# Forgetting attention and a tanh-shrink MLP on one core: half-feature order for unit 0, a subtraction on GpSimd, merged selectors, a q copy on VectorE and one step moved

## The chip, the cores and the metric

The kernel runs on one core of a Trainium2 chip. The metric is the device time of one execution in microseconds (us). Times inside an execution are counted from the start of the profiled span. Engines: PE is TensorE (PEld its weight loads), DVE is VectorE, ACT is ScalarE, POOL is GpSimd, SP is SyncE. A trailing q (SPq, POOLq) is the engine's sequencer, which issues DMAs.

## What is computed

Eight batches of eight heads, 576 positions, head size 64, in float32. The output of the attention becomes rows of 512 features for a two-layer MLP.

```python
scores = scale * q @ k.T                       # scale = 1/8
cum    = cumsum(log(clip(f, 1e-4, 1)))         # per head, over positions
scores = where(causal, -1e9, scores + cum[i] - cum[j])
attn   = softmax(scores)                       # rows divided by sum + 1e-9
x      = (attn @ v) as [4608, 512]             # batch and position, head and feature
h      = x @ w_in                              # 2048 features
out    = (h - tanh(h)) @ w_out                 # [4608, 512]
```

## The kernel before

**Order.** Each engine executes its instructions in the order in which the program writes them; the order is written by hand. The attention goes by pairs of heads of one batch (32 pairs, numbered 0 to 31; pairs 0 to 3 are batch 0, 4 to 7 batch 1), and the MLP by units of 512 rows (9 units, 0 to 8). The loop at the end of the kernel makes pass p: att_items(p) lists the attention's work for pair p, its seven score tiles t0 to t6 with what goes between them, and the loop puts TAKE[p] steps of the MLP between these items, as evenly as they go. Pass p also holds the values of pair p - 1, behind its tile t2.

**Scores and decay.** scores() makes one tile in a PSUM bank: a product over 67 rows, of which 64 are head features and three carry the decay, so that PE adds cum[i] - cum[j]. These three rows hold a high part (chi) and a low part (clo) of cum for the keys, a shifted cum (cq) for the queries, and constant rows of ones (ones16) and of a negative constant (minus16), against which chi and clo are multiplied. They reach the head layouts QT and KT by small DMAs: bulk() issues those of batch 0 on GpSimd (k_hi, q_hi and k_lo), load_aug() the others on SP. Pair 0 does not wait for them; it has its own layouts QS and KS, whose 88 rows include selector rows made from the columns of `per` (isb, isc, mul_*, add_*). Behind the product ScalarE takes the exponential of the tile (L367) into e; from batch 1 on GpSimd zeroes the part above the diagonal (L377, the mask). From batch 1 on the tiles use two PSUM banks in turn (ps_sc). Tile t3 takes the last keys of both heads, into el.

**Layouts of q and k.** trans() turns a pair's q or k on PE (L304) and copies the halves into QT and KT by VectorE and ScalarE (L317, L315). For pair 0 it is called with split=True, with four smaller copies (64x288); two are done at once and two returned as functions (q_rest, k_rest), which start() calls later. From batch 3 on, q and k are turned by DMA transposes on SP instead.

**Values.** values() multiplies the tiles with v (L395), VectorE divides (L404 to L406) into xn, and turn() brings xn into the MLP's layout XR: by PE in batch 0 (L423), by two DMA transposes on SP from batch 1 on (L429, L431). weights() prepares sums of quarters of w_out on VectorE (L284) in passes 8 to 10.

**MLP.** mlp1 makes 128 of the 2048 features for the 512 rows of a unit (L457, four products over 128 features of x, the last of which needs the last pair's xn), ScalarE takes the tanh (L462) and VectorE adds (L468) into gq. Unit 0's second product is mlp2_plain: sixteen steps s0 to s15, each eight products (L498) over one half of the features for 128 rows and half of the output. Four steps share one PSUM bank, which ScalarE copies (L503) and SP sends to memory. The later units use mlp2. Unit 1's first step needs xn of pairs 4 to 7.

**The start.** start() prepares pair 0. unread(n) makes n products of a constant tile that nobody reads. `late` holds the causal constants of batch 0, which PE adds to the scores (L361). The GpSimd queue also issues all loads of q, k, v, w_in (win) and w_out (wout), between its masks.

The step's order and the passes' shares before the change:

```python
e, mp, m, half = s // 8, s // 4 % 2, s // 2 % 2, s % 2
...
TAKE = (0, 0, 0, 0, 2, 7, 6, 6, 6, 8, 8, 7, 7)
```

Of the kernel before, what the change touches and what calls it, by code (L numbers as in the profile page):

```python
# [11 lines left out]
ALU = mybir.AluOpType  # L12
# [4 lines left out]
SHIFT = 5.0  # L17
# [4 lines left out]
def kernel(  # L22
# [10 lines left out]
    nc = tc.nc  # L33
# [3 lines left out]
    NH = B * H  # L37
# [7 lines left out]
    inv_qscale = float(D) ** 0.5  # L45
# [47 lines left out]
    qn, kn = ([t[0:S // NT6, :].rearrange("p (h n d) -> p h n d", h=H, n=NT6) for t in raw] for raw in (qraw, kraw))  # L93
# [42 lines left out]
    NX = NH + 3 * H  # L136
# [7 lines left out]
    id16 = cst.tile([P, P], FP16)  # L144
# [7 lines left out]
    ones16 = TK[0:NX, 0, :]  # L152
    nc.vector.memset(ones16, 1.0)
    minus16 = TK[0:2 * H, 1, :]
    nc.vector.memset(minus16, -1.0)
    late = cst.tile([P, P], FP16)
    nc.vector.memset(late, 0.0)
    nc.vector.memset(KT[0][:, :, S:PITCH], 0.0)
    chi = cst.tile([NX, S], FP16)
    clo = cst.tile([NH, S], FP16)  # L160
    cq = cst.tile([NH, S], FP16)
    KS = W1.rearrange("p k e -> p (k e)")[:, 0:2 * PITCH].rearrange("p (a n) -> p a n", a=2)
    QS = W2.rearrange("p k e -> p (k e)")[:, 0:2 * S].rearrange("p (a n) -> p a n", a=2)
    nc.vector.memset(KS[0:NX, :, S:PITCH], 0.0)
    per = cst.tile([NX, 9], FP32)
    nc.vector.memset(vn[0][D:P, NJ - 1, :, :], 0.0)
    isb, isc, mul_k, add_k, mul_l, mul_0, add_0, mul_1, add_1 = (per[:, i:i + 1] for i in range(9))
    EL = [cst.tile([P, 192], FP16, tag=f"el{i}", name=f"el{i}") for i in range(3)]
    load_v_rest(0)
    load_v_head(0, 0)  # L170
# [1 line left out]
    nc.gpsimd.affine_select(out=late, in_=late, compare_op=ALU.is_ge, fill=-60000.0,  # L172
                            base=0, pattern=[[1, P]], channel_multiplier=-1)

    def column(g, h):
        return id16[0:NX, NH + 3 * h + g:NH + 3 * h + g + 1]

    for to, g in ((isb, 1), (isc, 2)):
        nc.vector.tensor_reduce(out=to, in_=id16[0:NX, NH + g:NX:3], op=ALU.add, axis=mybir.AxisListType.X)
    nc.vector.tensor_scalar(out=mul_k, in0=isb, scalar1=-inv_qscale, scalar2=inv_qscale, op0=ALU.mult, op1=ALU.add)  # L180
    nc.vector.tensor_scalar_mul(out=add_k, in0=isb, scalar1=-1.0)
    nc.vector.tensor_scalar_mul(out=mul_l, in0=isc, scalar1=inv_qscale)
    for e in EL[0:2]:
        nc.vector.memset(e, 0.0)
    nc.vector.tensor_scalar(out=lf, in0=lf, scalar1=0.0001, scalar2=1.0,
                            op0=ALU.max, op1=ALU.min)
    nc.vector.memset(vn[0][:, :, :, D:VW], 1.0)
    for h, (mul, add) in enumerate(((mul_0, add_0), (mul_1, add_1))):
        nc.vector.tensor_scalar_mul(out=mul, in0=column(1, h), scalar1=inv_qscale)
        nc.vector.scalar_tensor_tensor(out=add, in0=mul, scalar=-SHIFT, in1=column(0, h), op0=ALU.mult, op1=ALU.add)  # L190
        nc.vector.tensor_tensor(out=add, in0=add, in1=column(2, h), op=ALU.subtract)
    nc.scalar.activation(out=lf, in_=lf, func=AF.Ln)
    nc.scalar.activation(out=expo, in_=lf[0:1, 0:1], func=AF.Exp)
    cum = TQ[0][0:NX, :, :].rearrange("p c s -> p (c s)").bitcast(FP32)[:, S:2 * S]
# [20 lines left out]
    def bulk():  # L215
        (k_hi, chi_0), (k_lo, clo_0), (q_hi, cq_0) = aug_rows(0)
        load_qk(qn, q, 0, 4, 6)
        load_qk(kn, k, 0, 4, 6)
        nc.gpsimd.dma_start(out=k_hi, in_=chi_0)
        nc.gpsimd.dma_start(out=q_hi, in_=cq_0)  # L220
        nc.gpsimd.dma_start(out=k_lo, in_=clo_0)
        load_qk(qn, q, 0, 6, H)
        load_qk(kn, k, 0, 6, H)
        for n in range(NJ - 1):
            load_v_block(0, n, 2, H)
# [264 lines left out]
        nc.vector.tensor_tensor(out=LHS[name](u, i)[:, ks], in0=LHS[x](u, i)[:, ks], in1=LHS[y](u, i)[:, ks], op=op)  # L490

    def mlp2_plain(u, s):
        e, mp, m, half = s // 8, s // 4 % 2, s // 2 % 2, s % 2
        if s % 4 == 0:
            M2[u] = bank("ops").rearrange("p (m e) -> p m e", m=2)
        ops, t0 = M2[u], (2 * mp + m) * P
        for ft in range(half * NK, half * NK + NK):
            nc.tensor.matmul(out=ops[:, m, :], lhsT=GQ[(u, ft % NK // 4)][:, half, ft % 4, t0:t0 + P],  # L498
                             rhs=wout[:, ft, e * HE:(e + 1) * HE], start=(m == 0 and ft == 0),
                             stop=(m == 1 and ft == NFT - 1), skip_group_check=True)  # L500
        if s % 4 == 3:
            ost = tmp.tile([P, DM], FP32, tag="ost", name="ost", bufs=3).rearrange("p (m e) -> p m e", m=2)
            nc.scalar.activation(out=ost, in_=ops, func=AF.Copy)  # L503
            r0 = u * UW + mp * 2 * P
            nc.sync.dma_start(out=out[r0:r0 + 2 * P, e * HE:(e + 1) * HE].rearrange("(m p) e -> p m e", p=P), in_=ost)
# [63 lines left out]
    def unread(n, lent=False):  # L569
        idle = m_bank("idle") if lent else ps_tr.tile([P, UW], FP32, tag="tr", name="idle")  # L570
        for i in range(n):
            nc.tensor.matmul(out=idle[:, i % 4 * P:i % 4 * P + P], lhsT=warm, rhs=warm, start=True, stop=True)
# [5 lines left out]
    def start():  # L578
        def row_q(h, mul, add):
            nc.scalar.activation(out=QS[NH:NX, h, :], in_=cum[NH:NX, :], func=AF.Identity, bias=add[NH:NX, :], scale=mul[NH:NX, :])  # L580

        unread(47)
        row_q(0, mul_0, add_0)
        q_rest = trans(*pairs[0], qn, (QS,), True, "AAAA", True)
        nc.scalar.activation(out=cq, in_=cum[0:NH, :], func=AF.Copy, bias=-SHIFT * inv_qscale, scale=inv_qscale)
        unread(6)
        k_rest = trans(*pairs[0], kn, (KS,), True, "VVVV", True)
        unread(38)
        q_rest[0]()
        scores(*pairs[0], 0)  # L590
        unread(4)
        nc.vector.scalar_tensor_tensor(out=clo, in0=cum[0:NH, :], scalar=inv_qscale, in1=chi[0:NH, :], op0=ALU.mult, op1=ALU.subtract)
        nc.vector.tensor_copy(out=KS[NH:NX, 1, 0:S], in_=KS[NH:NX, 0, 0:S])
        for fn in k_rest:
            fn()
        scores(*pairs[0], 1)
        row_q(1, mul_1, add_1)
        unread(4)
        q_rest[1]()
# [7 lines left out]
    def att_items(p):  # L607
        def put(fn, *args):
            items.append((lambda: fn(*args), True))

        items = []
        here = pairs[p] if p < len(pairs) else None
        before = pairs[p - 1] if 0 < p <= len(pairs) else None
        after = pairs[p + 1] if p + 1 < len(pairs) else None
        early = p < NPAIR
        for ti in range(len(TILES)):
            if here and (p > 0 or ti > 1):
                put(scores, *here, ti)
            if p == 1 and ti == 6:
                items.append((lambda: const_rows(1), False))  # L620
                items.append((lambda: load_aug(1), False))
            if p == 0 and ti in (0, 2, 5, 6):
                put(unread, {0: 2, 2: 14, 5: 4, 6: 6}[ti])
            if p == 1 and ti == 6:
                put(unread, 8, True)
            if p == 1 and ti == 3:
                put(last)
            for load in LOADS.get((p, ti), ()):
                items.append((load, False))
            at_q, at_k = (1, 3) if p == 0 else (0, 1) if early else (0, 2) if p == NPAIR else (0, 3)  # L630
            if p in (2 * NPAIR - 1, 2 * NPAIR, 2 * NPAIR + 1) and (ti % 2 or ti == 0):
                items.append((rest, False))
            if p in (2 * NPAIR - 1, 2 * NPAIR) and ti % 2 == 0:
                pair = pairs[2 * NPAIR + 2 * (p - 2 * NPAIR + 1) + ti // 4]
                put(trans, *pair, *((kn, KT) if ti % 4 else (qn, QT)), False, "VA")
            if ti == at_q and p < 2 * NPAIR - 1:
                put(trans, *after, qn, QT, early, "VV")
            if p == NPAIR:
                if ti in (4, 5):
                    put(mlp1, 0, ti - 4, 1)  # L640
            if ti == at_k and p < 2 * NPAIR - 1 and p != NPAIR:
                put(trans, *after, kn, KT, early, "AV" if early and p > 1 else "VV")
            if p == NPAIR:
                if ti == 1:
                    put(turn, *pairs[p - 2])
                    put(values, *before)
                    put(mlp1, 0, 0, 0)
                elif ti == 2:
                    put(mlp1, 0, 1, 0)
                    put(turn, *before)  # L650
                    put(trans, *after, kn, KT, early, "VV")
            elif early and ti in (2, 4) and before:
                put(values, *before, (ti // 2 - 1,))
            elif not early and ti == 2 and before:
                put(values, *before, (0, 1), p == NPAIR + 2)
            if p < NPAIR:
                if ti == 1 and p > 1:
                    put(turn, *pairs[p - 2], True)
            elif p > NPAIR and ti == 3:
                items.append((release, False))  # L660
                put(turn, *before)
        return items
# [1 line left out]
    mlp = [(mlp1, u, s) if s < NFT else (mlp2_plain if u < PLAIN else mlp2, u, s - NFT)  # L664
           for u in range(NU) for s in range(2 * NFT if u < PLAIN else NFT + 2 * len(STEPS))]
    mlp = mlp[2:]
    TAKE = (0, 0, 0, 0, 2, 7, 6, 6, 6, 8, 8, 7, 7)
    at = 0
    start()
    bulk()  # L670
# [56 lines left out]
```

## Time and profile before

| | |
|---|---|
| median of 3 runs | 341.16 us (341.16 to 341.31) |
| profiled execution | 341.6 us, span 339.9 us |
| granted TensorE clock | 1.000 |
| PE busy | 333.0 us, 98% of the span |
| VectorE busy | 262.5 us, 77% |
| ScalarE busy | 235.1 us, 69% |
| GpSimd busy | 163.7 us, 48% |
| chain that ended last | PE 85%, DVE 8%, DMA 2%, ACT 2%, issue 1% |

The profile is one execution. The page gives busy times per engine, the chain of work that ended last, and groups of instructions by line of the kernel. The trace behind it answers what was done in a stretch, what an engine waited for, and when a DMA was issued and landed. An engine's share is a mean over stages with different limits, so the stage around a change has to be read by itself.

### The profile page before, as it was taken

The page shows a single profiled execution, that of the slowest core. Times are in us where ns is not written, and L with a number is a line of the kernel's source. Part 1 is how long each engine was busy: PE and PEld are TensorE (multiplying, and loading weights), DVE is VectorE, ACT ScalarE, POOL GpSimd, SP SyncE. Part 2 cuts the span into 40 slices and gives each one's busy share as a digit, 9 for nine tenths or more (in the row PEclk, how much of TensorE's full clock was granted, in tenths as well). Part 3 has the DMA queues.
Part 4 walks back from the last instruction along what each step waited for, and adds up shares of the span by engine and source line. Part 5 has one row for each costly group of instructions (what it writes and reads, how often), then busy time and mean ns, then how long its engine had stood idle before and what let it go on. Part 6 is the DMA issues. An engine that isn't in the chain of part 4 may idle for free.

```text
span 339.9 us, 8804 instructions
## 1 busy us (share of the span) xinstructions
PE 333.0 (98%) x3345; PEld 237.7 (70%) x3345; DVE 262.5 (77%) x516; ACT 235.1 (69%) x440; POOL 163.7 (48%) x323
## 2 busy tenths in 40 slices
PE   8999999999999999999999999999999999999995
PEld 8775557875588558855788888656875686486485
DVE  8898986659888888678967886688668766966864
ACT  6998777878987886778677867787558743632630
POOL 8894765885657573677377647632322210000000
PEclk9999999999999999999999999999999999999999
DMA  9999999999959999999999999990130023002003
GB/s 116 124 173 201 187 198 179 153 162 196 137 93 181 159 116 92 136 168 130 106 106 191 131 110 112 165 133 15 49 115 13 17 62 101 0 31 95 1 16 109
DMA packets 147535, 38.88 MB, mean 114 GB/s; under 512 B 128221, under 2 KB 146381, under 8 KB 147493
## 3 DMA queue, kind: packets, MB, share of 16 engines
q0 software_dynamic: 94592, 18.39, 74.1%
q1 hardware_dynamic: 52868, 19.88, 31.7%
q8 instruction: 26, 0.43, 0.5%
q14 instruction: 17, 0.13, 0.2%
q10 hardware_dynamic: 32, 0.06, 0.0%
HBM read 36.90 MB, written 9.44 MB: 136 GB/s over the span
## 4 chain that ended last, share of the span: by engine, by line
PE 85%; DVE 8%; DMA 2%; ACT 2%; issue 1%; ACTq 0%
PE hps L457 35%; PE ops L523 29%; PE ps L358 11%; PE av L395 7%; DMA XR<-xn 2%; PE ops L498 2%; DVE KT L317 2%; DVE QT L317 1%; ACT e L367 1%; DVE gq L468 1%; PE t L304 1%; DVE xn L406 1%; DVE W L317 1%; PE x L423 0%; DVE TQ L195 0%
## 5 line engine op out<-in xcount | busy, mean ns | idle before, releaser
L457 PE MATMUL hps<-XR,win 128*128 128x512 f16 (+1 forms) x640 | 140.9, 357 | 0.5 <-DMA XR<-xn 0.3
L462 ACT ACTIVATE th<-hps 128x512 f32<-128x512 f32 x144 | 86.6, 602 | 55.5 <-PE hps L457 52.8
L367 ACT ACTIVATE e<-ps 128x512 f16<-128x512 f32 x192 | 110.5, 598 | 9.8 <-PE ps L358 7.9
L468 DVE TENSOR_TENSOR gq<-hps,th 128x512 f16<-128x512 f32 x144 | 98.1, 687 | 24.2 <-ACT th L462 22.6
L377 POOL TENSOR_SCALAR_AFFINE_SELECT e<-e 128x128 f16<-128x128 f16 x168 | 60.3, 362 | 69.9 <-ACT e L367 67.9
L457 PEld LDWEIGHTS <-win 128*128 128x128 f16 x640 | 57.7, 97 | 48.7 <-issue 0.7
L358 PE MATMUL ps<-QT,KT 67*128 67x512 f16 (+1 forms) x372 | 73.8, 277 | 0.8 <-ACT e L367 0.4
L523 PEld LDWEIGHTS <-gq 128*128 128x128 f16 x640 | 60.2, 97 | 11.2
L523 PE MATMUL ops<-wout,gq 128*128 128x256 f16 x512 | 63.2, 272 | 0.0
L358 PEld LDWEIGHTS <-KT 67*128 67x128 f16 x372 | 35.3, 98 | 22.2 <-issue 1.2
L395 PEld LDWEIGHTS <-e 128*128 128x128 f16 x896 | 32.3, 97 | 3.6
L395 PE MATMUL av<-vn,e 128*128 128x65 f16 x896 | 33.6, 193 | 0.0
L131 POOL DMA_DIRECT2D vn<-in_v_dram x32 | 28.0, 878 | 7.5 <-DMA win<-in_moe_w_in_dram 3.4
L523 PE MATMUL ops<-W,sq 128*128 128x256 f16 x256 | 31.2, 272 | 0.0
L406 DVE TENSOR_TENSOR xn<-av,rs 128x640 f16<-128x640 f32 x32 | 26.4, 825 | 1.1
L523 PEld LDWEIGHTS <-sq 128*128 128x128 f16 x256 | 24.1, 97 | 3.4
L108 POOL DMA_DIRECT2D qn<-in_q_dram x25 | 21.1, 845 | 3.7 <-DMA wout<-in_moe_w_out_dram 1.9
L377 POOL TENSOR_SCALAR_AFFINE_SELECT el<-el 128x128 f16<-128x128 f16 x28 | 9.4, 337 | 26.9 <-ACT el L367 26.7
L108 POOL DMA_DIRECT2D kn<-in_k_dram x25 | 21.1, 845 | 1.5 <-issue 1.1
L404 DVE TENSOR_SCALAR rs<-av 128x10 f32<-128x10 f32 x32 | 5.2, 162 | 18.1 <-PE av L395 17.0
L498 PE MATMUL ops<-wout,gq 128*128 128x256 f16 x128 | 16.9, 272 | 0.4 <-DVE gq L468 0.3
L317 DVE COPY QT<-t 64x576 f16<-64x576 f16 x18 | 14.4, 801 | 3.5 <-PE t L304 3.4
(93 smaller groups left out, 321.0 us busy)
## 6 DMA issues: line engine op xcount, KB each, us to landing
out_dram<-ost SPq DMA_DIRECT2D x34, 256.0 KB
vn<-in_v_dram POOLq DMA_DIRECT2D x24, 128.0 KB, 5.6
qn<-in_q_dram POOLq DMA_DIRECT2D x20, 128.0 KB, 4.9
kn<-in_k_dram POOLq DMA_DIRECT2D x20, 128.0 KB, 5.0
win<-in_moe_w_in_dram POOLq DMA_DIRECT2D x2, 1024.0 KB, 12.3
wout<-in_moe_w_out_dram POOLq DMA_DIRECT2D x2, 1024.0 KB, 17.0
XR<-xn SPq DMA_TRANSPOSE x56
qn<-in_q_dram POOLq DMA_DIRECT2D x6, 144.0 KB, 4.7
```

The source lines that it names most:

```text
L108: nc.gpsimd.dma_start(out=dst[b % 2][0:pn, n, :].rearrange("p (h d) -> p h d", h=H), in_=src[b, :, n * P:n * P + pn, :].rearrange("h p d - ...
L131: nc.gpsimd.dma_start(out=vn[b % 2][:, n, h0:h1, 0:D], in_=v[b, h0:h1, n * P:(n + 1) * P, :].rearrange("h p d -> p h d"))
L317: nc.vector.tensor_copy(out=to, in_=of)
L358: nc.tensor.matmul(out=ps[:, col:col + n], lhsT=kt[0:rows, h, j * P:(j + 1) * P], rhs=qt[0:rows, h, i0:i0 + n], start=True, stop=cut == 0)
L367: nc.scalar.activation(out=e[:, lo:hi], in_=ps[:, lo:hi], func=AF.Exp, scale=qscale)
L377: nc.gpsimd.affine_select(out=view, in_=view, compare_op=ALU.is_ge, fill=0.0, base=0, pattern=pat, channel_multiplier=-1)
L395: nc.tensor.matmul(out=av[:, a, ib, :], lhsT=E.pop((b, c, a, j, ib)), rhs=vn[b % 2][:, j, 2 * c + a, 0:D + 1], start=(j == 0), stop=(j == ib))
L406: nc.vector.tensor_tensor(out=xn.rearrange("p i (a d) -> p a i d", a=2), in0=av[:, :, :, 0:D], in1=rs.to_broadcast([P, 2, NJ, D]), op=ALU. ...
L457: nc.tensor.matmul(out=hps[:, o:o + n], lhsT=win[:, ci, ft * P:(ft + 1) * P], rhs=XR[:, ci, t:t + n], start=(ci == 0), stop=(ci == NCH - 1))
L462: nc.scalar.activation(out=th, in_=hps, func=AF.Tanh, scale=-1.0)
L468: nc.vector.tensor_tensor(out=GQ[(u, i)][:, half, kt, :], in0=hps, in1=th, op=ALU.add)
L523: nc.tensor.matmul(out=ps[:, m, :], lhsT=LHS[lhs](u, kt // 4)[:, kt % 4, m * P:(m + 1) * P], rhs=rhs[:, kt, :], start=(fresh and (apart or ...
```

## The change

- **Halves.** In mlp2_plain the two lowest digits of the step number change their meaning: within a bank, s0 and s1 now read the first half of the features for both groups of rows, s2 and s3 the second half.
- **Low decay part.** clo is computed on GpSimd as cum - chi, between the issues of k_hi and q_hi, and no longer on VectorE in start(). For this chi and clo of the heads are no longer scaled by sqrt(64) = 8: mul_k is 1 in these rows (one memset more), and the constant row minus16 is -8 in place of -1.
- **Selectors.** The rows mul and add of both heads are computed together, in three operations on two columns in place of six on one.
- **q copy.** The last of pair 0's four q copies goes to VectorE ("AAAV"), and the third is called behind the first scores in place of ahead of them, so ScalarE takes the first exponential first.
- **Idle products.** unread makes 36 in place of 38 ahead of the first scores, and 9 in place of 14 at tile t2 of pass 0.
- **One step.** Pass 8 takes five MLP steps in place of six, and pass 11 eight in place of seven. In PE's order s9 goes from just ahead of pair 7's values to just behind them; the steps after it are one place later until pass 11. Unit 0's third output transfer on SP goes behind the five DMA transposes of batch 3's q.

```diff
-    nc.vector.memset(minus16, -1.0)
+    nc.vector.memset(minus16, -inv_qscale)
...
-    isb, isc, mul_k, add_k, mul_l, mul_0, add_0, mul_1, add_1 = (per[:, i:i + 1] for i in range(9))
+    isb, isc, mul_k, add_k, mul_l, mul_0, mul_1, add_0, add_1 = (per[:, i:i + 1] for i in range(9))
...
-    def column(g, h):
-        return id16[0:NX, NH + 3 * h + g:NH + 3 * h + g + 1]
...
+    nc.vector.memset(mul_k[0:NH, :], 1.0)
...
-    for h, (mul, add) in enumerate(((mul_0, add_0), (mul_1, add_1))):
-        nc.vector.tensor_scalar_mul(out=mul, in0=column(1, h), scalar1=inv_qscale)
-        nc.vector.scalar_tensor_tensor(out=add, in0=mul, scalar=-SHIFT, in1=column(0, h), op0=ALU.mult, op1=ALU.add)
-        nc.vector.tensor_tensor(out=add, in0=add, in1=column(2, h), op=ALU.subtract)
+    mul, add = per[:, 5:7], per[:, 7:9]
+    of = [id16[0:NX, NH + g:NH + g + 4:3] for g in range(3)]
+    nc.vector.tensor_scalar_mul(out=mul, in0=of[1], scalar1=inv_qscale)
+    nc.vector.scalar_tensor_tensor(out=add, in0=mul, scalar=-SHIFT, in1=of[0], op0=ALU.mult, op1=ALU.add)
+    nc.vector.tensor_tensor(out=add, in0=add, in1=of[2], op=ALU.subtract)
...
         nc.gpsimd.dma_start(out=k_hi, in_=chi_0)
+        nc.gpsimd.tensor_tensor(out=clo, in0=cum[0:NH, :], in1=chi[0:NH, :], op=ALU.subtract)
         nc.gpsimd.dma_start(out=q_hi, in_=cq_0)
...
-        e, mp, m, half = s // 8, s // 4 % 2, s // 2 % 2, s % 2
+        e, mp, half, m = s // 8, s // 4 % 2, s // 2 % 2, s % 2
...
-        q_rest = trans(*pairs[0], qn, (QS,), True, "AAAA", True)
+        q_rest = trans(*pairs[0], qn, (QS,), True, "AAAV", True)
...
-        unread(38)
+        unread(36)
+        scores(*pairs[0], 0)
         q_rest[0]()
-        scores(*pairs[0], 0)
         unread(4)
-        nc.vector.scalar_tensor_tensor(out=clo, in0=cum[0:NH, :], scalar=inv_qscale, in1=chi[0:NH, :], op0=ALU.mult, op1=ALU.subtract)
...
-                put(unread, {0: 2, 2: 14, 5: 4, 6: 6}[ti])
+                put(unread, {0: 2, 2: 9, 5: 4, 6: 6}[ti])
...
-    TAKE = (0, 0, 0, 0, 2, 7, 6, 6, 6, 8, 8, 7, 7)
+    TAKE = (0, 0, 0, 0, 2, 7, 6, 6, 5, 8, 8, 8, 7)
```

## The prediction

> **What bounds the kernel now.** I read the page's engine shares first, then PE's busy time by stretches, the list of what PE waited for, the chain that ended last with the work named, and at last GpSimd's timeline (POOL) against ScalarE's (ACT).
>
> ```profile
> PE 333.0 (98%) x3345; PEld 237.7 (70%) x3345; DVE 262.5 (77%) x516; ACT 235.1 (69%) x440; POOL 163.7 (48%) x323
> ```
> ```profile
> 0.00:20.00 20.00, 18.23 (x263) 1.00 1.12 124
> 20.00:50.00 30.00, 29.15 (x351) 1.00 1.40 194
> 50.00:76.00 26.00, 25.21 (x311) 1.00 2.19 164
> 76.00:180.00 104.00, 104.00 (x995) 1.00 1.44 135
> ```
> The columns of the second view are the stretch, its length, PE's busy time and its instructions, the granted clock, the DMA share and GB/s. From 76 us on PE has no gap and keeps the full clock, so work that only changes place behind 76 us is worth nothing. All that the change can win or lose is how early PE gets past 76 us.
>
> ```profile
> PE ps L358 <- ACT e L367: 0.6, 2, 0.4
> PE ops L498 <- DVE gq L468: 0.3, 1, 0.3
> PE hps L457 <- DMA XR<-xn: 0.3, 1, 0.3
> ```
> ```profile
> 9.08 0.76 DVE clo L592
> 14.47 0.39 PE ps L358
> 52.61 1.20 DVE gq L468 x2
> 53.81 0.05 issue
> 53.86 0.28 PE ops L498
> 67.83 7.57 DMA XR<-xn
> 75.40 0.04 issue
> 75.45 0.38 PE hps L457
> ```
> The first of these is what PE waited for (us in total, times, longest), the second the chain in order of time (start, us, what). Three places of the chain belong to the change: VectorE's run of copies up to 14.43, in which clo stands; step s1 of unit 0, which waits for the last two gq; and the first product of unit 1, which waits for the transposed xn of pair 7. The idle spans understate the two waits, since a matmul is drawn past the start of the next one. By starts: s1's matmuls should follow 0.11 apart (eight in 0.88), but the last three starts lose 0.25 and 0.49, so 0.74 in all; the fourth hps matmul came at 75.45 where its three forerunners would have put it at 75.01, so 0.44.
>
> ```profile
> 9.40 0.53 POOL L220 DMA_DIRECT2D QT<-cq  x1 [0.78 <-ACT cq L585]
> 10.12 0.51 POOL L221 DMA_DIRECT2D KT<-clo  x1 [0.19 <-issue]
> 10.62 0.65 POOL L102 DMA_DIRECT2D qn<-in_q_dram  x1
> 60.48 0.88 POOL L108 DMA_DIRECT2D qn<-in_q_dram  x1 [1.89 <-DMA wout<-in_moe_w_out_dram]
> 63.43 1.44 POOL L377 TENSOR_SCALAR_AFFINE_SELECT e<-e 128x256 f16<-128x256 f16 x2
> ```
> GpSimd has a hole before 9.40, and from 10.62 it issues loads without one. At 60.48 it waits for a load issued eight loads earlier (wout, landed 60.18), and the masks of pair 7 queue behind that: t6's mask is the first of the two at 63.43, 1.20 of them, against 0.43 for the mean mask of its size, while VectorE's weight step ran beside it (63.70 to 64.36).
>
> **The start.** Of six selector operations three go: on the chain they hold 4.80 to 5.24, 0.44. One memset comes, 0.07 (as for late and W), ahead of the clamp of lf; so Ln would end at 5.01 in place of 4.94, and the scan can start near 5.05, not 5.25: -0.20. VectorE loses clo (-0.76) and takes a 64x288 copy (+0.48): -0.28. Together pair 1's first scores come 0.48 earlier than 14.47. ScalarE must follow: exp of t0 now stands ahead of a q copy (0.49) and waits for scores instead (0.45 of idle); the later q copy is gone. So exp of t2 starts at 11.84 instead of 12.10 and pair 1's first exp near 14.50 instead of 14.96: -0.46. The seven idle matmuls taken out (57 ns each) stood ahead of PE waits of 0.31 and 0.22: nothing.
>
> **GpSimd's subtraction.** No row shows a two-input operation there. The masks cost 327 ns at 128 columns and 433 at 256, so 0.83 ns a column over 0.22 us. With 576 columns and the second input free that is 0.70; with the second input at full price (1152 columns) 1.18; with the slowing of the mask at 63.43 (1.20 for 0.43) on 0.70, 1.95. I take 1.18, since both inputs must be read. [...] The subtraction begins at 8.66, after k_hi's issue; q_hi is issued at 9.84 (cq is ready by then), k_lo at 10.37, and the load that stood at 10.62 comes at 10.88. So every later load is 0.26 late (0.22 early at 0.70, when cq decides; 1.03 late at 1.95). k_lo landed 2.56 after its issue, so now near 12.95, needed at 14.0: hidden.
>
> That delay has two takers. The first half of win landed at 28.31 and PE used it at 28.91. Landing at 28.57 lets PE start at 28.62 (0.05 as at 75.40): of the 0.46 only 0.29 is left.
>
> **Halves.** s1 now reads the first features with the second rows, and the last two gq, ready at 53.81, are needed at the end of s2, 0.9 later: +0.74. Together 1.03 ahead at that place. Here DMAs do not bind: kn of batch 2 landed at 53.61 (now 53.87) and is used at 55.55 - 1.03 = 54.52.
>
> **The moved step.** Pair 7's values come one step, 0.87, earlier still. They read t6's mask at 66.00; now they would at 66.00 - 0.87 - 1.03 = 64.10. Masks follow the wout landing: 60.74, then 2.95 as before, then an undisturbed 0.42 make 64.11. VectorE's weight step moves with PE to about 62.7 and meets t5's mask; the mask that began inside such a step at 68.10 took 0.45 for 0.30, so 0.15 more, and 0.06 to wake PE: 64.32. PE waits 0.22 (0.85 if 0.78 is lost as at 63.43).
>
> Next ScalarE. From pair 8's t4 to pair 9's t1 PE had 4.01 (67.25 to 71.26); one step less leaves 3.13. In between ScalarE does exp t4, exp t5, output copy, QT copy, exp t6. t4's exp starts 0.47 after its scores; 0.60 + 0.58 + 0.13 (waiting for s11) + 0.60 + 0.84 + 0.62 put the end at 3.84. t1 needs the bank that t6's exp frees (there are two), so PE waits 0.70; before, 0.12 was in hand. Queued behind this exp are t0's exp, a KT copy and exps t1 and t2, needed only by pair 9's values, two steps later.
>
> The transposes landed 9.06 after pair 7's values ended (66.34 to 75.40); now the product that reads them comes 8.67 + 0.87 = 9.54 after: the wait of 0.44 is gone. An output DMA also moves on SP behind five transposes (7.5 us); ost has three buffers, so nobody waits. In pass 11, where PE is full, the extra step is the same work.
>
> **Sum.** 0.29 + 0.74 - 0.22 - 0.70 + 0.44 = 0.55. The profiled execution was 341.6 (span 339.9 and 1.7 around it) and becomes 341.05; the timed median is 0.44 lower, 341.16, and becomes 340.6. A difference under 0.2%, 0.68 us, is about what a measurement here cannot tell from none.
>
> **Rivals.** (a) No new waits in pass 8: ScalarE's copies or the masks are taken earlier than I count. For: 0.22 hangs on 0.3 us of mask, and exps may overlap by 0.1, as at 69.08. Against: ScalarE was idle only 0.5 in 60.4 to 74.25. It gives 0.29 + 0.74 + 0.44 = 1.47: 339.7.
> (b) The transposes land by the DMA backlog, not by their issue: at 75.40 again. The same work lies before and after that product, so all gains end there: 341.2. For: the DMA share is 2.19 in that stretch. Against: the four pairs turned between 41 and 70 all took 6.8 to 7.7 from issue to last packet.
> (c) The subtraction is slow and holds the load queue: slower. Each us of it delays win and wout by one, so the sum is 0.55 - (T - 1.18): nothing at T = 1.73, and 0.68 slower at 2.41; at 3.0, 342.4. For: mask and load issue share the engine, and the mask at 63.43 was nearly tripled beside VectorE. Against: VectorE's operations beside it are mostly copies from PSUM, and memsets beside such copies at 19.7 ran at 1.0 ns a column. [...]
>
> **How the numbers follow.** Forecast 0.47, holding gains of 0.1 to 0.95, two in five of it above 0.68; (a) 0.30; (b) 0.09; (c) 0.14, nearly all of it slower by over 0.68. Faster 0.19 + 0.30 = 0.49, rounded to 0.50; slower 0.13; same 0.37. The range leaves out (a)'s far end and most of (c): 339.6 to 341.5.
>
> **What would show it.** Right: clo on GpSimd for about 1.2 ending near 9.9; pair 1's first scores near 14.0; win landing at 28.6 with PE at once; no gq wait at s1; a PE wait on exp at pair 9's t1 and none on XR. Wrong: clo over 1.7, PE reaching 28.9 later than before, or an XR wait that stays.

## The result, and the profile after

The kernel became slower: 345.22 us against 341.24 in the median (345.1 to 346.4 in 4 runs; 341.16 to 341.38), a ratio of 1.0124 with a 95% interval of 1.0102 to 1.0147. The forecast was 340.6. The profiled execution took 345.11 us, span 343.4.

PE by stretches of the kernel after; the columns are those of the same view of before, and the last two rows cut the third one finer:

```profile
0.00:20.00 20.00, 17.25 (x253) 1.00 1.11 124
20.00:50.00 30.00, 29.08 (x351) 1.00 1.40 192
50.00:76.00 26.00, 23.13 (x261) 0.93 2.15 163
76.00:180.00 104.00, 104.00 (x1016) 1.00 1.52 132
68.00:72.00 4.00, 1.24 (x15) 1.00 2.40 177
72.00:76.00 4.00, 4.00 (x23) 0.57 2.47 139
```

Between 20 and 50 us and behind 76 almost nothing changed. In the first 20 us PE is busy 0.98 us less, but it makes idle products there, and it comes out of the start only 0.2 us later (below). The loss is in two neighbouring stretches: from 68 to 72 us PE is busy for 1.24 of 4 us, and from 72 to 76 it is busy all the time, but at a granted clock of 0.57. The third row's clock of 0.93 is the mean that hides this. The same two stretches before:

```profile
68.00:72.00 4.00, 4.00 (x45) 1.00 2.41 189
72.00:76.00 4.00, 3.73 (x53) 1.00 2.40 121
```

What PE waited for, after:

```profile
PE ops L498 <- ACT KT L315: 2.8, 1, 2.8
PE ps L358 <- ACT e L367: 0.6, 2, 0.4
PE ps L358 <- DVE KT L317: 0.5, 1, 0.5
```

One wait of 2.8 us is new: an MLP product (ops) waits for a copy of k on ScalarE. The waits for gq and for XR are gone, as forecast. The third row is new too, and belongs to the start. So does a new wait of 0.6 for a load of q, not shown, which costs nothing: the transposes behind it start at 5.79 us, 5.76 before. The chain through the loss, after (start, us, what):

```profile
67.91 0.56 PE ops L498 x5
68.47 0.02 issue
68.50 0.23 ACT ost L503
68.73 0.39 issue
69.12 0.09 ACT QT L315
69.21 0.74 issue
69.95 1.09 ACT e L367 x2
71.03 0.02 issue
71.06 0.81 ACT KT L315
71.87 0.04 issue
71.91 1.78 PE ops L498 x8
```

The eight products of s12 start at 71.91, as soon as the copy of KT ends, and they take 1.78 us where a step takes 0.88: from the third on their starts are 213 ns apart instead of 109.

**Why a product of the MLP waits for a copy of k.** Three PSUM banks (m0 to m2) serve the products of the MLP, and m_bank deals them out in turn. From pass 7 on one of them is set aside for the transposes of batch 2's k; at pass 9 the loop gives it back:

```python
def m_bank(name):
    while M_AT[0] % 3 in KEPT:
        M_AT[0] += 1
    ...
def keep():                         # called at pass 7
    ...
    KEPT.append(M_AT[0] % 3)
...
elif KEPT and src is kn:            # in trans()
    t32 = ps_m.tile([P, UW], FP32, tag=f"m{KEPT[0]}", name="t32")
...
if p == 2 * NPAIR + 1:              # pass 9
    KEPT.clear()
```

Followed through the program, unit 0's four banks were 0, 2, 0, 2 before. s12, which opens the fourth, was the last step of pass 8, bank 1 was still set aside, and s12 took bank 2. With five steps in pass 8, s12 is the first step of pass 9, behind KEPT.clear(), and the banks are 0, 2, 0, 1. Bank 1 holds the k of pair 11, transposed by PE at 68.52, and its copy stands on ScalarE behind an output copy, a q copy and two exponentials, at 71.06. The first product of s12 has to wait until the bank is read, and all that PE has queued waits with it: 2.93 us more than the usual distance of two starts.

**The sum, as it came.** Lateness of PE against before, from the two profiles: first hps product 29.12 for 28.91, +0.21; step s1 without its wait, -0.74, so 0.53 ahead at pair 9's first tile (68.77; 70.17 before with one step, 0.87, more in front of it). Then the wait, +2.93; the half clock, +1.66 (from pair 9's first tile to the first hps product 9.71 us pass, and 8.05 in the profile of e3 below, which has the same wait at the full clock); and no wait for XR, -0.44. The total is 3.62; the times differ by 345.11 - 341.6 = 3.51, so 0.1 is left unexplained.

### The profile page after: what moved, and what is told of

It reads as the page before. It is cut to its first block, busy times and chain, and to the rows that moved or that the text cites. A ratio compares the mean times of both kernels' runs of the same rounds, so it can differ in the third digit from the quotient of the medians.

```text
span 343.4 us, 8787 instructions
## 1 busy us (share of the span) xinstructions
PE 333.4 (97%) x3338; PEld 237.8 (69%) x3338; DVE 262.1 (76%) x514; ACT 234.2 (68%) x439; POOL 165.3 (48%) x324
## 4 chain that ended last, share of the span: by engine, by line
PE 91%; DVE 5%; ACT 2%; issue 1%; ACTq 0%
PE hps L457 36%; PE ops L523 29%; PE ps L358 12%; PE av L395 8%; PE ops L498 4%; ACT e L367 2%; DVE KT L317 1%; PE t L304 1%; DVE QT L317 0%; DVE TQ L194 0%; PE x L423 0%; PE idle L572 0%; ACT KT L315 0%; DVE W L317 0%; DVE xn L406 0%
## 5 line engine op out<-in xcount | busy, mean ns | idle before, releaser
L523 PE MATMUL ops<-wout,gq 128*128 128x256 f16 x512 | 63.1, 272 | 0.0
L498 PE MATMUL ops<-wout,gq 128*128 128x256 f16 x128 | 18.0, 288 | 2.8 <-ACT KT L315 2.8
L538 ACT ACTIVATE m<-ops 128x512 f32<-128x512 f32 x16 | 9.6, 597 | 11.2 <-PE ops L523 11.2
```

What stands on the lines that cost most here:

```text
L523: nc.tensor.matmul(out=ps[:, m, :], lhsT=LHS[lhs](u, kt // 4)[:, kt % 4, m * P:(m + 1) * P], rhs=rhs[:, kt, :], start=(fresh and (apart or ...
```

## The experiments

Each was timed beside the kernel before on the same chip; the median of before was 341.29 to 341.44 in these.

**The moved step back, and the moved step alone.**

```diff
# e1, from the kernel after
-    TAKE = (0, 0, 0, 0, 2, 7, 6, 6, 5, 8, 8, 8, 7)
+    TAKE = (0, 0, 0, 0, 2, 7, 6, 6, 6, 8, 8, 7, 7)
# e3, from the kernel before
-    TAKE = (0, 0, 0, 0, 2, 7, 6, 6, 6, 8, 8, 7, 7)
+    TAKE = (0, 0, 0, 0, 2, 7, 6, 6, 5, 8, 8, 8, 7)
```

> The changed kernel with the passes' shares of before (pass 8 takes six steps, pass 11 seven), all other edits kept. Theory A, the step's bank: with s12 in pass 8 again, its PSUM bank is chosen while the bank of k's transposes is still set aside; the PE wait of 2.76 us near 69 us and the half clock behind it are gone. At pair 9's first tile the changed kernel was 0.53 us ahead of before at equal work, and the wait for XR stays, so 340.7 us. Theory B, ScalarE is simply late in pass 8 (the order of its copies): the wait shrinks but stays above 1 us, 342 or more.

> The kernel before with the one step moved and nothing else. Theory A: s12 gets the bank of k's transposes here too: a PE wait of about 2.8 us near 70 us, half clock for some 3.5 us behind it, 341.2 + 2.9 + 1.6 - 0.4 = 345.3 us. Rival C, the loss belongs to the whole (the halves or the later start push the step into the wait): at most 342.

e1: 341.47 (340.88 to 342.54, 10 runs; 340.7 was expected), ratio 1.0006 (0.9995 to 1.0017). e3: 345.01 (344.1 to 347.24, 4 runs), ratio 1.0119 (1.0080 to 1.0158). The wait for the copy is gone in e1 and whole in e3, so the moved step carries the loss, and all other parts together are worth nothing that can be measured.

**Another bank for s12.** One line at KEPT.clear() makes m_bank skip bank 1, from the kernel after (e2) and from before with the moved step (e8).

```diff
             KEPT.clear()
+            M_AT[0] += 1
```

> The changed kernel, step moved as it is, but the counter of the PSUM banks goes on by one where the set-aside bank is given back, so that s12 takes the bank after it. No instruction changes its place. Theory A: no wait on the KT copy, the clock stays full; 340.3 us if nothing else waits (0.53 ahead, XR wait of 0.44 gone), 341.0 if the ScalarE wait of 0.7 at pair 9's t1 exists that the prediction priced. Theory B: the order of the queues is the same, so 345.2 again.

> The kernel before with the one step moved and the counter of the PSUM banks put on by one, so that s12 takes a free bank. Theory A: no wait on the KT copy and no half clock. What is left is the step's price by the prediction: XR wait of 0.44 gone, a wait of 0.7 on ScalarE's exponential at pair 9's t1, so 341.5 us. Rival, the step is worth something by itself: 340.8 or less.

e2: 342.92 (341.3 to 344.95, 10 runs), ratio 1.0048 (1.0027 to 1.0068). e8: 342.01 (341.88 to 342.85, 11 runs), 1.0019 (1.0011 to 1.0028). The wait for the copy is gone in both: the bank was its cause, not the place of the step. e8 shows what the move costs without the bank: a wait at pair 9's tile t1, 0.74 from start to start. The chain of e2 has the same:

```profile
70.32 0.60 ACT e L367
70.92 0.04 issue
70.97 0.38 PE ps L358 x2
```

PE waits for t6's exponential, which holds one of the two score banks: the term that the prediction put at 0.70. e2 did not reach 340.6, though. Its largest waits:

```profile
PE ops L523 <- DVE ost L542: 1.5, 1, 1.5
PE ps L358 <- ACT e L367: 1.1, 3, 0.6
```

The first is at 107.7 us, where before had no gap. VectorE, which PE waits for there, was late from 96.5 us on (timeline of e2; in brackets its idle time before, and what ended it):

```profile
96.51 0.45 DVE L120 COPY KT<-TK 64x1152 f16<-64x1152 f16 x1 [2.75 <-DMA TK<-kn]
```

VectorE stood 2.75 us for the transposed k of batch 3. Its loads landed at 79.36 (76.82 before), but SP began to issue the transposes only at 82.64 (81.95 before), so the landing of the loads alone does not explain the wait. Before, this copy began at 94.40 without a wait. A second transfer was as late: the chain of e2 has the transposes of an earlier pair's xn land at 97.33, where VectorE's next xn begins (95.20 before), so without the wait for k VectorE would have stood there. What PE had gained came back as waits on transfers; which of the two set the time is not shown.

**The wait filled.** Fifty idle products in a free bank, ahead of s12 of the kernel after, so that PE works while it waits.

```diff
+        if s == 12:
+            M_AT[0] += 1
+            unread(50, True)
+            M_AT[0] -= 2
```

> The changed kernel with 50 idle products in the free bank put ahead of s12, which still takes the bank of k's transposes. The wait for the KT copy stays. Theory D, the idle of 2.76 us itself makes the clock drop to half from 72 to 75.6 us, which costs about 1.6 us: with PE busy the granted clock stays at 1.0 and the time is 343.6 us. Rival, the clock drops for another reason, or the slow matmuls are slow by their bank: 345.2 us.

343.45 (343.44 to 343.48, 4 runs), ratio 1.0064 (1.0049 to 1.0079). PE by stretches, e4:

```profile
68.00:72.00 4.00, 4.00 (x65) 1.00 2.41 174
72.00:76.00 4.00, 4.00 (x59) 1.00 3.00 91
```

The clock stays at 1.00 and 345.22 - 343.45 = 1.77 us are back, though the copy is awaited as before. Of the loss, some 1.7 us were the half clock behind the wait and not the wait.

**Halves alone.** From the kernel before:

```diff
-        e, mp, m, half = s // 8, s // 4 % 2, s // 2 % 2, s % 2
+        e, mp, half, m = s // 8, s // 4 % 2, s // 2 % 2, s % 2
```

> The kernel before with unit 0's new half order alone. Theory: the 0.74 us that s1 lost waiting for the last two gq are gone and PE stays ahead, 340.5 us. Rival, later waits on transfers (the transposed xn of pair 7 near 75 us, the transposed k of batch 3 near 95 us) come at their own time and take it back: 341.2 us.

341.27 (340.58 to 342.47, 12 runs), ratio 0.9991 (0.9978 to 1.0004): no difference that can be measured. The gq wait is gone and its 0.74 us are won at s1. Five of the twelve executions, at 340.58 to 340.88, seem to keep the gain. In the profiled one (341.66) it is lost again 20 us later; the chain of e5:

```profile
67.15 8.34 DMA XR<-xn
75.48 0.04 issue
75.53 0.38 PE hps L457
```

Pair 7's transposes were issued at 67.15 instead of 67.83, and landed at 75.48 instead of 75.40. PE's wait there grew from 0.44 to 1.21.

**The start: clo alone, and the copy out of its way.** e6 is the kernel before with clo on GpSimd (and the factor of 8 moved into the constants, as in the change). e7 is the kernel after with the step back and the key row's copy behind k_rest.

```diff
# e7
-        nc.vector.tensor_copy(out=KS[NH:NX, 1, 0:S], in_=KS[NH:NX, 0, 0:S])
         for fn in k_rest:
             fn()
+        nc.vector.tensor_copy(out=KS[NH:NX, 1, 0:S], in_=KS[NH:NX, 0, 0:S])
```

> The kernel before with clo on GpSimd (and the scale moved into the constant row), nothing else. Theory E: VectorE's copy of the 24 key rows (L593, 0.30 us before) stands beside the GpSimd subtraction and waits for its end, 0.9 us as in the changed kernel, so of the 0.76 saved only about 0.17 is left at pair 1's first scores (14.3 in place of 14.47), and the loads come 0.17 to 0.2 later: 341.2 to 341.6 us. Rival, the copy was slow there for another of the edits: it takes 0.30 and pair 1's first scores come near 13.7.

> The changed kernel with the passes' shares of before, and VectorE's copy of the key rows called behind the two key copies, when the subtraction on GpSimd has ended. Theory E: the copy takes 0.30 us again and pair 1's first scores come near 14.1 us in place of 14.70. In the end it is worth nothing where win's landing near 29 us and the transposes of batch 3 set the time: 341.4 us, as with the copy in its place; if they do not, 340.8.

Timeline of the kernel after, GpSimd and VectorE:

```profile
8.53 1.31 POOL L219 TENSOR_TENSOR clo<-TQ,chi 64x576 f16<-64x576 f32 x1
```
```profile
9.12 0.89 DVE L592 COPY W<-W 24x576 f16<-24x576 f16 x1
```

The copy took 0.30 before. Beside GpSimd's subtraction it ends 0.17 to 0.18 after it: 0.89 here and 0.91 in e6 (subtraction 8.62 to 9.93, copy 9.20 to 10.11). In e7 it stands at 10.10, behind the subtraction, and takes 0.30 again. So VectorE gave 0.75 of clo away, and its copy took 0.59 more. e6: 341.33 (341.25 to 342.15, 11 runs), ratio 1.0002 (0.9993 to 1.0010); its first scores of pair 1 come at 14.57, not at 14.3. e7: 341.8 (340.29 to 343.46, 12 runs), ratio 1.0015 (0.9997 to 1.0033); the copy is free, but VectorE now waits 0.75 for a q copy of ScalarE, and the first scores of pair 1 come at 14.97. The start was not mended by it, and a scatter of 3 us makes its time say little.

**Where the gains go.** If PE's lead comes back as waits because the DMA engines have a backlog, fewer transfers must let it stand. Three kernels leave out the same loads.

```diff
         for n in range(NJ):
-            if n < NJ - 1:
+            if b == 2:
+                pass
+            elif n < NJ - 1:
                 add(at_v[n], load_v_block, b, n, 0, H)
```

> The kernel before, without the five loads of batch 2's v (issued 46 to 52 us, landed 61 to 65 us; its values then multiply batch 0's v, so the output is not the reference's). Theory (from about 30 to 90 us the DMA engines have a backlog, and what PE gains ahead of it comes back as a wait on a later transfer): batch 3's k, which landed at 76.8, lands some us earlier; the 0.44 us wait for the transposed xn near 75 goes, and the median falls from 341.3 to about 340.9. Rival (these waits follow from the place of the instructions in their queues): the wait stays and the median is 341.2 to 341.4.

> The kernel before with the halves alone, and again without the loads of batch 2's v. Theory (backlog): the halves take 0.74 at step s1, and with the loads gone nothing takes it back near 74, where the wait had grown from 0.44 to 1.21: 341.3 - 0.74 - 0.44 = 340.1, so 0.7 below the run with the loads gone and nothing else changed. Rival: the wait of 1.2 stays near 74, the median is about 341.3.

> The changed kernel with the other bank for s12, without the loads of batch 2's v. Theory (backlog): VectorE no longer waits 2.8 us for batch 3's k before 96.5, PE's wait of 1.66 near 107 is gone; the waits left are ScalarE's 0.74 at pair 9's t1 and, ahead of the loads left out, up to 0.5 for win. From before: -0.74 (gq) + 0.74 (exp) - 0.44 (transposed xn) + 0.1 to 0.6 (start and win) gives 340.9 to 341.4, with a scatter much below that of 341.3 to 345. Rival (VectorE's order): the median stays near 342.9 and the wait near 107 is still there.

e9: 341.35 (341.08 to 341.96, 11 runs). e10: 340.42 (340.37 to 340.54, 6 runs), ratio to before 0.9970 (0.9959 to 0.9981), and 0.93 below e9. e11: 341.33 (341.24 to 341.82, 11 runs), 1.6 below e2, with a scatter of 0.6 instead of 3.7 us; VectorE's copy is back at 93.70 without a wait, and PE's wait at 107 is gone. With these loads gone, the halves bring what they were forecast to bring (0.74 at s1; another 0.17 between the profiled executions of e9 and e10 is an earlier start), and the moved step costs what its ScalarE term says. Batch 3's k landed at 73.6 to 75.3 in these. Leaving loads out also shortens GpSimd's queue, which issues them. That the DMA engines matter is seen in pair 7's transposes, which SP issues: from issue to landing the first took 5.6 to 6.0 us in e9 to e11, and 6.3 to 8.3 in the ten profiles with all loads at their old place.

e9 missed its expectation in one point: the wait for XR is gone from its profile (341.32), yet its median is that of before. So the usual execution of before does not seem to have that wait; it was in the profiled one, 341.6, which lay 0.44 above the median of the first three runs and 0.16 to 0.36 above the later medians of before (341.24 to 341.44). e8 agrees: its profiled execution, without that wait, lies 0.28 above the profiled one of before, its median 0.69 above the median of before.

**A version that uses it.** Nothing is left out here: the kernel before, the halves, and batch 3's loads of k two tiles later.

```diff
-        at_k = [(p0, n) for n in range(NJ)]
+        at_k = [(p0, n + (2 if b == FAR else 0)) for n in range(NJ)]
```

> The kernel before with the halves, and batch 3's five loads of k issued two tiles of pass 8 later (some 2.5 us), so that fewer loads run beside pair 7's transposes (issued from 67, landed 75.3). Nothing is left out. Theory (backlog): the wait for the transposed xn, 1.21 us with the halves alone, falls to 0.4 or less; k, which landed at 76 to 79, lands near 79 and is still in time for SP's transposes at 82; the median is near 340.6. Rival (the transposes land late whatever is loaded beside them, or k now comes too late): the wait stays or VectorE waits for k near 94, and the median is 341.3 or more.

340.52 (340.36 to 341.0, 7 runs) against 341.44, ratio 0.9974 (0.9963 to 0.9985): faster than both kernels. PE's waits and its stretch from 50 to 76 us in e12:

```profile
PE idle L572 <- DVE warm L141: 1.1, 1, 1.1
PE ps L358 <- DVE rs L405: 0.4, 1, 0.4
PE hps L457 <- ACT XR L427: 0.2, 1, 0.2
```
```profile
50.00:76.00 26.00, 25.88 (x316) 1.00 2.07 168
```

Neither gq nor a transfer of XR is left among them, and the four products of unit 1 run from 73.59 without a gap. The loads were issued from 65.97 on instead of 64.14, and k landed at 77.50. Pair 7's first transpose took 6.81 from issue to landing, 8.34 in e5; but that is inside the 6.3 to 8.3 of the other profiles, so that the later loads made it shorter is likely from the medians and not shown by this one execution.

## Why the prediction was wrong

- **The moved step: the step that failed.** The prediction followed it through the SP queue, the masks, ScalarE's order, the output buffers and pass 11, but not through the banks that m_bank deals out. It counted the banks of the scores ("there are two") and none for the products, and so never met KEPT.clear(), across which s12 moved. Missing were +2.93 of waiting and some 1.7 of half clock: e3 has the wait from the moved step alone, and e1, e2 and e8, where s12 gets another bank, are without it. Nothing in a trace of before shows this wait; it could be seen only by writing down which bank each step takes.
- **ScalarE's exponential, 0.70:** right, 0.74 to 0.75 in e2, e8 and e11. In the changed kernel s12 stands in front of it and it does not appear.
- **The gq wait, 0.74:** right, wherever the halves are in. Whether it reaches the end is another matter (below).
- **The masks, 0.22:** not there. Pair 7's values began at 64.01 with no stall. GpSimd waited 0.63 for wout (1.89 in the profile of before) and then 1.01 for a load of v; t6's mask began at 62.72 (63.43 before), took 0.83 instead of 1.20 and ended at 63.55, ahead of the values. The sum had put its end at 64.11 at best.
- **The wait for XR, 0.44:** probably counted twice. It was taken as a gain, and again as the distance from the profiled execution to the median. It is gone from the profile after, but the median of before, as e8 and e9 indicate, had no such wait to lose.
- **The start, 0.46 of gain cut to 0.29:** the wrong sign, +0.23 at pair 1's first scores and +0.21 at the first hps product. GpSimd's subtraction was well estimated (1.18 for 1.31), but it was priced by itself. What it does to the VectorE copy beside it, 0.59, was not, though t6's mask of before, which took 1.20 beside VectorE's weight step against a mean of 0.43, pointed there. The scan, forecast 0.20 sooner, began later too: at 5.26 (5.17 before). The clamp of lf began 0.13 later and took 0.61 instead of 0.46, and Ln and the scan followed it. All seven profiles with the additional memset have the late clamp, but so has one of the seven without it: e9, whose start is that of before, has the clamp at 3.94 with 0.57, the scan at 5.36 and pair 1's first scores at 14.60. So part of the +0.23 may belong to the execution, and why the clamp is longer stays open. The merged selectors do save: e6, with six operations and the same late clamp, begins its scan at 5.36, 0.10 later.
- **win:** forecast 28.57, landed at 28.57, by chance. Other kernels with the same start have it at 27.54 (e4) and 29.62 (e1), so a shift of 0.26 could not be forecast, and PE's 0.56 for win in e1 is of the same scatter.
- **"Work that only changes place behind 76 us is worth nothing":** true for the profile of before alone. With PE ahead, e2 has a wait of 1.66 at 107.7 from start to start.
- **The rivals.** (a) assumed no new waits. (b), that transfers land by the backlog and end all gains, had 0.09. It did not set this result, but it is what the halves alone met: transposes issued 0.68 earlier landed 0.08 later. e9 to e11 show that the load on the DMA engines matters for it (5.6 to 6.0 us from issue to landing, against 6.3 to 8.3), and the median of e12 agrees. Against it the prediction set the time from issue to last packet of four earlier pairs; the page's line of DMA shares, 9 in each slice but one up to the 27th of 40, spoke for it. (c), a slow subtraction that holds the load queue, was wrong: k_lo and the loads behind it came 0.17 later.

Still open is why e1, e2 and e4, all with the start of the changed kernel and the halves, had batch 3's k land at 79 to 80 (79.53 in the kernel after), and halves alone at 76.8. The last of these loads was issued at 68.96 there and at 69.77 in the kernel after, 0.8 later, and landed 2.7 later. The edits alone do not make it so: e7, which has them too, issued that load at 68.81 and had k at 75.69.

## What to carry to other kernels

A step that is moved takes everything with it that the program hands out in turn: write down which bank, buffer or semaphore each step gets before and after the move, and above all whether it crosses a line that lends one out or takes it back. A wait that is removed is a gain only if the next thing that PE needs is early as well (in e5 0.74 was won at s1 and the median stayed, 341.27 for 341.32); when the DMA row is full, look at what the transfers behind it will do, and move loads apart before moving work forward (e12: 340.52 for 341.44). And do not take a profiled execution's wait as a gain if the median is below that execution by about that much.

## What the runs showed of the hardware

- **The clock after a wait.** In the kernel after, PE idle for 2.8 us was followed by a granted clock of 0.57 from 72 to 76 us, which cost 1.66 us against e3 and 1.77 against e4. It does not follow each time: the profiled execution of e3, 344.1 us, had the same wait and a mean clock of 1.000; those at 345.71 and 347.24, of which no trace is kept, had 0.994 and 0.989. With fifty idle products in the wait the clock stayed at 1.00 (e4). What decides whether the clock falls after such a wait no run here shows.
- **GpSimd beside VectorE.** VectorE's copy of 24x576 in f16 between two places of SBUF ended 0.17 to 0.18 after GpSimd's subtraction in the kernel after and in e6, 0.89 and 0.91 long instead of 0.30; its copies from PSUM of 64x288 just before it took 0.97 and 0.98 for two, as before, and four of them beside the subtraction of e7 took 1.99. The rows agree with a copy that is held until the subtraction ends; what would hold it no run here shows.
